# Early folds of the first batch's second row half on GpSimd, free PSUM banks for MLP groups, and transfers planned with other landings, in an attention and Fourier-mixing kernel on one core

## The chip, the cores and the metric

The kernel runs on one core of a Trainium2 chip. Such a core has five engines that run side by side, each with its own instruction queue and in its own order: TensorE (PE in the profile: matmuls, and PEld: its weight loads), VectorE (DVE), ScalarE (ACT), GpSimd (POOL) and SyncE (SP, which issues transfers). They wait for one another through semaphores. Transfers run on 16 DMA engines that all the queues share. Matrix products go into PSUM, which has eight banks per core; everything else lies in SBUF.

The metric is the time of one execution in device microseconds (us), shown as the median of several.

## The reference, cut to what matters

The inputs are `q`, `k`, `v` for 4 batches, 8 heads, 768 rows and 64 columns, memory keys and values of 8 rows for each head, and two MLP weights `w_ch1` (512 x 2048) and `w_ch2` (2048 x 512), all in float32.

```
for c in range(24):                      # chunks of 32 rows
    l, r = max(0, 32*c - 16), min(768, 32*c + 40)
    kk = concat(mem_k, k[:, :, l:r]); vv = concat(mem_v, v[:, :, l:r])
    a = softmax(q[:, :, 32*c:32*c+32] @ kk^T / 8)
    attn[:, :, 32*c:32*c+32] = a @ vv
x = attn as [4, 768, 512]
u = x + real(fft(fft(x, axis=1), axis=2))
un = (u - mean(u)) / sqrt(var(u) + 1e-6)          # over the 512 columns
out = u + relu(un @ w_ch1) @ w_ch2
```

So each batch goes through three stages: chunked attention, a two-dimensional discrete Fourier transform of which only the real part is kept, and a normalised MLP.

## The kernel before, in words

**Attention** (`attention(n)`) works on pairs of heads, four pairs to a batch, n = 0 to 15. For each pair GpSimd issues two transfers that load q and k and cast them to bf16 (`e_load_qk`, L324), into three buffers each (`qs`, `ks`); SP issues seven that load the values into one of four tiles `va` (`e_load_v`, L333, L337, L342). TensorE turns q and k with identity matmuls into PSUM (`turn`, L351; tiles `trq`, `trk`), ScalarE or, for k of the first batch, VectorE copies them out (`e_qT` L360, `e_kT` L379). Then, for two groups g of six 64-row blocks: scores (`e_scores`, L392, tile `sc`), exponentials (`e_exp`, L400, ScalarE), values with a column of ones for the sum (`e_values`, L416, tile `xa`, or `xo` in an MLP bank for g = 1 of the first batch), and division by the sum (`e_norm`, L426 and L427, VectorE), which writes rows 384g to 384g+383 of the pair's 128 columns of `xsb`, the batch's 768 x 512 result. With the pair order 0, 2, 1, 3 the columns c and 256 + c become ready early.

**The Fourier stage** uses symmetry: columns are folded (sums and differences of mirrored columns), the folded parts are split into an fp16 high part `hi` and a remainder `lo`, and products with cosine and sine tables transform the rows (tile `ps`) and then the columns (tile `pm`). The first batch has its own version, `first_fourier`, which starts on half the rows (g = 0: rows 0 to 383, g = 1: rows 384 to 767) before attention is complete. For each g and each parity `par`:

- `g_zy` (L556) adds or subtracts columns 0 to 127 and 256 to 383; it needs pairs 0 and 1 in order of work.
- `g_ff(..., last=0)` (L569, L571, L574), the early fold, twice per parity (`ab`), adds or subtracts the mirror of columns 128 to 255; it needs the third pair.
- `g_mid` (L600 to L603, GpSimd) prepares the middle columns; it needs the fourth pair. `g_row` (L608, L614) is its product.
- `g_ff(..., last=1)` (L573, L574), the last fold, with the fourth pair; then `g_hi` (L590, ScalarE), `g_lo` (L594, VectorE) and `g_rows` (L627, twelve matmuls).

`g_row(0)` is the first row transform that TensorE does. After g = 1 the results are copied out (`e_up` L500, `e_rest` L505, `e_dn` L513), `e_columns` (L638) transforms columns, `e_sum` (L644) adds x, `e_stats` (L652) and `e_un` (L658) normalise, and `e_turn_u` (L665) turns the result for the MLP. For the later batches (`fourier(b)`) GpSimd and SP send half of the rows through DRAM in mirrored order (`e_rows_out`, `e_rows_turn`, `e_mirror`), and SP turns the normalised rows by a transposing transfer (`e_flip`, L670).

**The MLP** takes half a batch (`sh`) at a time: 16 groups `e_ch1` (four matmuls into `ph`, L698), each followed by a ReLU on ScalarE (`e_relu`, L706), in order; then three groups `e_ch2` of 16 matmuls in four parts (`pc`, L713), and `e_osb` (L720) which adds u. The weights are eight GpSimd transfers (L906 for w1, L910 for w2), queued behind the loads of the sixth and the seventh head pair.

**PSUM.** The eight banks are handed out by name. The tags `acc` and `mlp` stand for two banks each; `tr`, `sc` (two banks) and `xa` hold the rest. Row and column transforms take `acc` (the first batch's rows of odd parity `mlp`). An MLP group has a fixed tag: `mtag` gives `acc` to every third one and `mlp` to the others.

**The order of the work** is made by a small planner, the class `Plan`, when the kernel is built. `add` notes a task with its engine, a cost in us, the tasks that it waits for (`after`, and `behind`: only issued later than that one), the buffers that it takes and gives back, and a rank. `order` then walks through a modelled time: whenever an engine is free, it takes the ready task of lowest rank. Without a rank given, a task's rank is its place in the list; MLP matmuls have a rank of a million and more, so they fill the holes of all other work. The result is a fixed order for each engine; on the chip an instruction waits for its real inputs, and everything behind it on its engine waits as well. Transfers with `moved` are modelled by `share`: the first transfer of each queue gets a share of the bandwidth, GpSimd's twice that of the others, and lands 2.8 us (GpSimd) or 1.4 us later, plus `late`.

While the first batch has no dense work for TensorE, the planner puts idle matmuls (`e_fill`, L771, operand `dz`) into its holes. A one-element copy, `e_gate` (L824), keeps GpSimd from issuing loads of the second batch before the fourth pair's values have landed.

GpSimd also prepares constants: zero rows of `kTb` (L777) and of `ks` (L754), masks, edges of `va` (L296 to L308). Their ranks run up to 17.1; those of the first three pairs' loads are given, up to 10.1, and the fourth pair's loads have their place in the list, which is higher than 20.

## Time and profile before

| quantity | value |
|---|---|
| median of 4 runs | 292.79 us (292.53 to 293.11) |
| the profiled execution's own time | 293.11 us |
| its span, first to last instruction | 291.4 us |
| PE busy, of the span | 94% |
| PE's first row transform (L608) | 32.44 us |
| PE's first MLP matmul (L698) | 55.12 us |
| PE's last matmul ends | about 287.2 us |

The span is what the trace shows; the device adds a little around it. A line of the order of time has the start and the duration in us, the engine, the line of the kernel, the operation, the result and its operands with their shapes, and how many were merged; in brackets how long the engine had been idle before it, and what ended that. A line of the waits has the waiting engine and line, what it waited for, the total in us, how often, and the longest. A line of the windows has the stretch, its length, then the busy time of PE, PEld, DVE, ACT and POOL with instruction counts, the granted clock, the DMA share and GB/s. Busy PE includes the idle matmuls of the start.

### The profile page before, as it was taken

How to read it: one execution, taken by the hardware profiler on the slowest of the kernel's cores; microseconds unless marked ns; L12 is line 12 of the kernel's file. 1: busy time of each engine (PE TensorE's matmuls, PEld its weight loads, DVE VectorE, ACT ScalarE, POOL GpSimd, SP SyncE). 2: the span in 40 equal slices, each digit the busy share in tenths (PEclk: the TensorE clock that was granted, in tenths of full speed). 3: DMA queues.
4: the chain of work that ended last, by engine and by line, in shares of the span. 5: the costliest groups of instructions: out<-in, count | busy, mean ns of one | idle time of the engine just before them, and what ended most of it. 6: DMA issues, size and time to landing. Idle time of an engine off the chain costs nothing.

```text
span 291.4 us, 7349 instructions
## 1 busy us (share of the span) xinstructions
PE 274.2 (94%) x3055; PEld 173.0 (59%) x3055; DVE 164.8 (57%) x354; ACT 164.7 (57%) x294; POOL 47.9 (16%) x96
## 2 busy tenths in 40 slices
PE   1599998998999999999999999999899999999994
PEld 1377697764566767566777646657554644645641
DVE  7979998941259874948885878864912012012011
ACT  5897356767576586877885246433750721712700
POOL 8824822310321010221010021010020000000000
PEclk9999999999999999999999999999999999999999
DMA  5998999997999967798940356944222504004204
GB/s 98 196 192 163 182 209 197 197 197 156 178 202 261 182 170 166 95 162 213 192 95 35 37 137 190 146 144 108 56 54 75 107 0 126 21 36 107 39 36 108
DMA packets 98689, 38.36 MB, mean 132 GB/s; under 512 B 85728, under 2 KB 93920, under 8 KB 98656
## 3 DMA queue, kind: packets, MB, share of 16 engines
q1 hardware_dynamic: 87344, 21.83, 39.9%
q0 software_dynamic: 10592, 15.21, 28.0%
q10 hardware_dynamic: 720, 0.85, 0.9%
q8 instruction: 24, 0.39, 0.6%
q14 instruction: 9, 0.07, 0.1%
HBM read 37.36 MB, written 13.37 MB: 174 GB/s over the span
## 4 chain that ended last, share of the span: by engine, by line
PE 78%; POOL 5%; DMA 5%; issue 4%; DVE 4%; SPq 2%; ACT 1%; POOLq 0%; DVEq 0%
PE pc L713 29%; PE ph L698 25%; PE xa L416 6%; PE ps L488 5%; PE pm L638 3%; DMA va<-in_mem_v_dram 3%; PE ps L627 2%; PE sc L392 2%; DMA qs<-in_q_dram 2%; SPq L333 2%; PE trq L351 2%; PE trk L351 2%; DVE st L652 1%; DVE xsb L644 1%; POOL qs L324 1%
## 5 line engine op out<-in xcount | busy, mean ns | idle before, releaser
L706 ACT ACTIVATE hT<-ph 128x384 f16<-128x384 f32 x128 | 60.8, 492 | 53.7 <-PE ph L698 52.8
L698 PE MATMUL ph<-unT,w_sb 128*128 128x384 f16 x512 | 88.9, 326 | 0.9 <-ACT hT L706 0.6
L713 PE MATMUL pc<-w_sb,hT 128*128 128x512 f16 x384 | 88.0, 380 | 0.0
L698 PEld LDWEIGHTS <-w_sb 128*128 128x128 f16 x512 | 48.4, 98 | 33.2 <-issue 1.8
L713 PEld LDWEIGHTS <-hT 128*128 128x128 f16 x384 | 35.8, 98 | 40.6 <-issue 0.4
L720 DVE SCALAR_TENSOR_TENSOR osb<-pc,rstd,xsb 128x512 f32<-128x512 f32 x24 | 18.0, 750 | 72.4 <-PE pc L713 69.7
L400 ACT ACTIVATE e<-sc,mbias 128x384 f32<-128x384 f32 x64 | 33.6, 578 | 10.6 <-PE sc L392 9.3
L416 PE MATMUL xa<-va,e 128*64 128x65 f32 x672 | 26.2, 228 | 0.8 <-DMA va<-in_mem_v_dram 0.8
L416 PEld LDWEIGHTS xa<-va,e 128*64 128x64 f32 x672 | 22.3, 139 | 7.8 <-issue 5.2
L658 ACT ACTIVATE un<-xsb,mu_s 128x512 f16<-128x512 f32 x24 | 17.2, 722 | 14.2 <-DVE mu_s L653 14.2
L500 ACT CAST up<-ps 128x386 f16<-128x386 f32 x16 | 9.7, 604 | 17.1 <-PE ps L488 15.6
L652 DVE BATCH_NORM_STATS2 st<-xsb 128x6 f32<-128x512 f32 x24 | 16.6, 690 | 0.7
L360 ACT COPY qT<-trq 128x768 bf16<-128x768 bf16 x16 | 12.7, 795 | 7.3 <-PE trq L351 7.3
L324 POOL DMA_DIRECT2D qs<-in_q_dram x16 | 10.6, 660 | 36.2 <-PE trq L351 22.9
L427 DVE TENSOR_TENSOR xsb<-xa,zs 128x384 f32<-128x384 f32 x28 | 15.6, 557 | 1.0
L505 DVE TENSOR_TENSOR up<-ps,up 128x386 f16<-128x386 f32 x16 | 9.5, 596 | 10.7 <-ACT up L500 10.7
L351 PE MATMUL trq<-ident_b,qs 96*64 96x96 bf16 x256 | 9.1, 218 | 6.7 <-DMA qs<-in_q_dram 6.7
L426 DVE RECIPROCAL zs<-xa 128x6 f32<-128x6 f32 x28 | 5.4, 191 | 17.1 <-PE xa L416 16.7
L379 ACT COPY kTb<-trk 128x1056 bf16<-128x1056 bf16 x12 | 12.5, 1040 | 2.2 <-PE trk L351 2.2
L324 POOL DMA_DIRECT2D ks<-in_k_dram x16 | 10.2, 640 | 20.8 <-PE trk L351 16.9
L644 DVE TENSOR_TENSOR xsb<-pm,xsb 128x512 f32<-128x512 f32 x15 | 10.1, 671 | 5.4 <-PE pm L638 5.4
L351 PEld LDWEIGHTS <-qs 96*64 96x64 bf16 x256 | 6.9, 116 | 10.1 <-DMA qs<-in_q_dram 7.6
(142 smaller groups left out, 331.2 us busy)
## 6 DMA issues: line engine op xcount, KB each, us to landing
va<-in_v_dram SPq DMA_DIRECT2D x32, 220.0 KB
w_sb<-in_moe_w_ch_dram POOLq DMA_DIRECT2D x8, 512.0 KB, 16.3
qs<-in_q_dram POOLq DMA_DIRECT2D x16, 192.0 KB, 6.0
ks<-in_k_dram POOLq DMA_DIRECT2D x16, 192.0 KB, 6.7
out_dram<-osb SPq DMA_DIRECT2D x12, 256.0 KB
x_rows<-xsb POOLq DMA_DIRECT2D x3, 768.0 KB, 5.0
xr<-x_back POOLq DMA_DIRECT2D x3, 768.0 KB, 5.3
out_rows<-osb SPq DMA_DIRECT2D x9, 256.0 KB
```

Source lines behind the costliest of these rows:

```text
L324: nc.gpsimd.dma_start(dst[n % NS][0:QP], src[b, 2 * pr:2 * pr + 2].rearrange("h (p j) d -> p h (j d)", j=RB))
L351: nc.tensor.transpose(out_[64 * hh:64 * hh + 64, j * w:(j + 1) * w], src[:, hh, j * D:(j + 1) * D], eye)
L400: nc.scalar.activation(e1[:, :, :, ts(half, 32)], sc[:, :, 0:6, ts(half, 32)], AFT.Exp, bias=mbias[:, half:half + 1], scale=1.0 / math.sqr ...
L416: nc.tensor.matmul(xa[64 * half:64 * half + 64, st, hh, 0:65], e1[:, hh, t6, :], v1[:, hh, 6 * g + t6, 0:65], start=True, stop=True)
L427: nc.vector.tensor_tensor(xs[b][:, 3 * g:3 * g + 3, 2 * pr * D:(2 * pr + 2) * D] .rearrange("p s (h d) -> p s h d", h=2), xa[:, :, :, 0:D] ...
L488: nc.tensor.matmul(out_[:, sp, :], part[:, ab, sp * 3 + st, c0:c1], tab[:, sp, st, :], start=(st == 0 and i == 0), stop=(st == 2 and i == 1))
L652: nc.vector.bn_stats(st6, xs[b][:, kt, :])
L658: nc.scalar.activation(un, xs[b][:, kt, :], AFT.Identity, bias=mu_of[b][:, kt, 0:1], scale=-1.0)
L698: nc.tensor.matmul(ph[:, 0:384], w1_sb[:, dt, ts(ht, P)], unT_of[b][:, dt, sh * 384:(sh + 1) * 384], start=(dt == 0), stop=(dt == NDT - 1))
L706: nc.scalar.activation(hT_of[b, sh][:, ht, :], ph[:, 0:384], AFT.Relu, bias=0.0, scale=-1.0)
L713: nc.tensor.matmul(pc_of[b, sh, stl], hT_of[b, sh][:, ht, ts(stl, P)], w2_sb[:, ht, :], start=(ht == 0), stop=(ht == NHT - 1))
L720: nc.vector.scalar_tensor_tensor(osb, pc, rstd_of[b][:, st:st + 1], xs[b][:, st, :], ALU.mult, ALU.add)
```

## The change: what it does

- **Early folds.** For g = 1, `g_zy` and `g_ff(..., last=0)` run on GpSimd: two `g_zy` and four early folds, with ranks 20.1 to 20.3 and costs of 1.1, 1.42 and 1.3.
- **Free banks.** An MLP group has no fixed tag. `order` picks, among `mlp` and `acc`, one that has a free bank, by how long it has been free.
- **Transfers.** `share` weighs each transfer by its own `grain` and slows small-grained ones to 0.85 beside others; `head` says after which part of its cost a transfer begins; `moved`, `late` and `grain` of value loads, weights, mirrored rows and outputs have new values. The transposing transfers `e_flip` are planned with a cost of 1.2 and a landing 1.6 later, and each goes behind the one before and no longer after it.
- **Tiles and a memset.** Two tiles `kU` (128 x 8 x 128, bf16) are new, and a GpSimd task `t_uz` with rank 20 and cost 0.4 that writes zeros to both.
- **A second way to load q and k**, with transposing transfers, for batches from `TURNED` on. `TURNED` is 9 and there are 4 batches.

```diff
     def __init__(self, slots):
-        self.free = dict(slots)
+        self.free = dict(slots, **{"": 0})
...
-            heads = [xs_[0] + [2.0 if q == "POOL" else 1.0] for q, xs_ in left.items() if xs_]
+            heads = [xs_[0] + [xs_[0][0]["grain"], q] for q, xs_ in left.items() if xs_]
             live = [h for h in heads if h[2] <= at + 1e-9]
             whole = sum(h[3] for h in live)
-            step = min([h[1] * whole / h[3] for h in live]
+            slow = {q: 0.85 if len(live) > 1 and xs_ and xs_[0][0]["grain"] < 0.05 else 1.0
+                    for q, xs_ in left.items()}
+            step = min([h[1] * whole / h[3] / slow[h[4]] for h in live]
...
-                    xs_[0][1] -= step * (2.0 if q == "POOL" else 1.0) / whole
+                    xs_[0][1] -= step * slow[q] * xs_[0][0]["grain"] / whole
...
-                    for tag in t["take"]:
+                    take = t["take"]
+                    if t["pick"] is not None:
+                        take += tuple(sorted((x for x in t["pick"]["of"] if self.free[x] > 0),
+                                             key=lambda x: (since.get(x, []) + [0.0])[0]
+                                             + t["pick"]["of"].index(x) * 0.5))[:1] or ("",)
+                    for tag in take:
                         need[tag] = need.get(tag, 0) + 1
...
-                        self.flow.setdefault(e, []).append([t, t["moved"], now + cost])
+                        self.flow.setdefault(e, []).append([t, t["moved"], now + cost * t["head"]])
...
-                        t["done"] = now + cost + self.LAG.get(e, 0.07)
+                        t["done"] = now + cost + (t["late"] or self.LAG.get(e, 0.07))
+                        if e == "SP":
+                            t["end"] = t["done"]
...
+    KR, KS, NKU = 16, 128, 2
+    kU = [spool.tile([P, RB, KS], BF16, name=f"kU{i}") for i in range(NKU)]
...
+    TURNED = 9
...
     def g_zy(par, g):
...
-        xb, sl = xs[0], slice(3 * g, 3 * g + 3)
-        nc.vector.tensor_tensor(zy_of[0, par][:, sl], xb[:, sl, 0:P], xb[:, sl, HD:HD + P],
+        xb, sl, eng = xs[0], slice(3 * g, 3 * g + 3), nc.gpsimd if g == 1 else nc.vector
+        eng.tensor_tensor(zy_of[0, par][:, sl], xb[:, sl, 0:P], xb[:, sl, HD:HD + P],
                                 ALU.add if par == 0 else ALU.subtract)
...
     def g_ff(par, ab, g, last):
...
+        eng = nc.gpsimd if g == 1 and not last else nc.vector
...
-    def mtag(b, i):
-        return "acc" if i % 3 == 2 else "mlp"
+    pick_of = {}
+
+    def pick(*key):
+        return pick_of.setdefault(key, dict(of=("mlp", "acc")))
...
-        ph_of[b, sh, ht] = ph = bank(mtag(b, ht), [P, 512], FP32, "ph")
+        ph_of[b, sh, ht] = ph = bank(pick(b, sh, ht)["tag"], [P, 512], FP32, "ph")
...
+    t_uz = add("POOL", 0.4, lambda: [nc.gpsimd.memset(kU[i], 0.0) for i in range(NKU)], rank=20)
...
         lv = add("SP", 2.5, lambda: e_load_v(n), [t_ones[n] if n < NV else None],
                  behind=t_x2.get(b - 2),
-                 take=("va",), moved=2.7, late=LATE if b else 0.0)
+                 take=("va",), moved=2.6, grain=0.031, head=0.4, late=(0.0, 4.0, LATE, LATE)[b])
...
-                w1_sb[:, dt, :], moe_w_ch1[ts(dt, P), :]), moved=2.55,
+                w1_sb[:, dt, :], moe_w_ch1[ts(dt, P), :]), moved=2.4, grain=0.32, late=2.0,
...
-                w2_sb[:, ts(g, 4), :], w2v[:, ts(g, 4), :]), moved=3.1,
+                w2_sb[:, ts(g, 4), :], w2v[:, ts(g, 4), :]), moved=2.6, late=2.0,
...
-                zy = add("DVE", 0.5, lambda par=par, g=g: g_zy(par, g),
+                early = ("DVE", "POOL")[g]
+                zy = add(early, (0.5, 1.1)[g], lambda par=par, g=g: g_zy(par, g),
                          [t_norm[0, g], t_norm[1, g], t_sines],
-                         take=("unT",) if g == 0 else ())
+                         take=("unT",) if g == 0 else (), rank=20.1 if g else None)
                 for ab in range(2):
-                    pre[par, ab, g] = add("DVE", 0.62 if ab == 0 else 0.5,
+                    pre[par, ab, g] = add(early, (0.62 if ab == 0 else 0.5) + 0.8 * g,
                                           lambda par=par, ab=ab, g=g: g_ff(par, ab, g, 0),
-                                          [zy, t_norm[2, g]],
+                                          [zy, t_norm[2, g]], rank=20.2 + 0.1 * par if g else None,
...
-                t_un[kt] = add("SP", 0.1, lambda kt=kt: e_flip(b, kt),
-                               [un, t_un.get(kts[i - 1]) if i else None],
-                               take=("unT",) if i == 0 else (), give=("un",), moved=0.8,
+                t_un[kt] = add("SP", 1.2, lambda kt=kt: e_flip(b, kt),
+                               [un], behind=t_un.get(kts[i - 1]) if i else None,
+                               take=("unT",) if i == 0 else (), give=("un",), late=1.6,
...
-                         take=(mtag(b, ht),), give=("unT",) if sh == 1 and ht == NHT - 1 else (),
+                         pick=pick(b, sh, ht), give=("unT",) if sh == 1 and ht == NHT - 1 else (),
```

## The prediction

> **What bounds the kernel now.** I read the page's busy shares first, then PE's waits, then windows by stage, then the order of time on PE and GpSimd from 7 to 33 us.
>
> ```profile
> PE 274.2 (94%) x3055; PEld 173.0 (59%) x3055; DVE 164.8 (57%) x354; ACT 164.7 (57%) x294; POOL 47.9 (16%) x96
> ```
>
> TensorE is busy for 94% of the span; no other engine passes 60%. The windows (PE busy first) say where the rest lies:
>
> ```profile
> 22.00:32.00 10.00, 9.70 (x204) 6.72 (x196) 9.36 (x25) 6.19 (x11) 5.77 (x13) 1.00 0.91 160
> 32.00:44.00 12.00, 12.00 (x159) 10.63 (x153) 11.49 (x32) 6.58 (x13) 5.82 (x10) 1.00 1.09 207
> 44.00:72.00 28.00, 26.07 (x390) 18.73 (x383) 17.33 (x42) 19.80 (x39) 4.84 (x8) 1.00 1.13 190
> 72.00:200.00 128.00, 128.00 (x1589) 81.76 (x1588) 90.20 (x170) 80.13 (x139) 15.74 (x22) 1.00 0.80 153
> 200.00:210.00 10.00, 9.11 (x65) 5.90 (x63) 7.82 (x18) 5.72 (x12) 0.00 (x0) 1.00 0.28 67
> ```
>
> From 32 us on TensorE has almost no gap: 1.93 us between 44 and 72, 0.89 between 200 and 210. Its waits from 30 us to the end name them:
>
> ```profile
> PE sc L392 <- ACT e L400: 0.8, 1, 0.8
> PE xa L416 <- DMA va<-in_mem_v_dram: 0.8, 1, 0.8
> PE ph L698 <- ACT hT L706: 0.6, 1, 0.6
> PE ph L698 <- DVE xsb L548: 0.3, 1, 0.3
> ```
>
> So two things count: when TensorE comes to its dense work, and these few waits. Before 32 us part of "busy" is idle filler (L771), and the dense work begins with the first row transform at 32.44. What leads there, in order of time on TensorE:
>
> ```profile
> 20.96 0.54 PE L351 MATMUL trq<-ident_b,qs 96*64 96x96 bf16 x16
> 21.32 0.54 PE L351 MATMUL trk<-turn_b,ks 100*64 100x100 bf16 x16
> 21.80 0.35 PE L392 MATMUL sc<-qT,kTb 64*128 64x64 bf16 x12
> 22.07 0.92 PE L416 MATMUL xo<-va,e 128*64 128x65 f32 x24
> ...
> 32.44 0.33 PE L608 MATMUL ps<-dz 128*128 128x386 bf16 x1
> ```
>
> The turns at 20.96 and 21.32 belong to the fourth head pair. GpSimd issues its loads here (with the memset rows that I price by):
>
> ```profile
> 7.30 0.78 POOL L777 MEMSET kTb<- 128x384 bf16 x2
> 9.33 1.99 POOL L754 MEMSET ks<- 4x1024 bf16 x2
> 14.97 0.13 POOL L308 MEMSET va<- 8x2 f32 x1
> 15.23 0.65 POOL L324 DMA_DIRECT2D qs<-in_q_dram  x1
> 15.88 0.63 POOL L324 DMA_DIRECT2D ks<-in_k_dram  x1
> ```
>
> Their landings, by tile, are 5.0 us (q) and 5.4 us (k) after issue: 20.2 and 21.28. So k arrives 0.04 us before TensorE turns it.
>
> **The change part by part.**
>
> *Dead code.* `TURNED = 9` with four batches: no branch on it runs, so the transposed q and k loads do not exist. What remains of it is two tiles, `kU`, and their memset, `t_uz`.
>
> *`t_uz` on GpSimd.* Rank 20 puts it behind the value-tile edges (17.1), which end at 15.10, and ahead of the fourth pair's loads, whose rank is their place in the list, far above 20. Nothing holds it back. It writes 128x1024 bf16 twice; the plan is told 0.4 us. By L754 (0.95 to 1.10 us for 1024 elements) the two take 1.9 to 2.2; by L777 (0.39 for 384) 2.1. A lower bound is VectorE's memset of `ks`, 0.485 for 1024 elements written as uint32: 0.97. I take 2.0, the same engine's row for the same length. The loads then go out at 17.23 and 17.88 and land at 22.2 and 23.3. TensorE, in order, turns k at 23.3 and not 21.32: +1.96. Behind it stand scores, values and 24 fillers whose number the plan, told 0.4, has no reason to change; ScalarE cannot hide it, since its exponentials wait 0.83 us each for `sc`. So the first row transform starts at about 34.4. Price: +1.96, all on the path.
>
> *Six early folds of rows 384 to 767 to GpSimd.* VectorE is rid of one fold at L556 (0.48, among three in 1.49) and of 2.6 us between 34.87 and 37.47: 3.1 together. On the path this is worth nothing, because TensorE is dense from 32.44 to 43.67 and would do no row transform sooner; the cover is gone only if that stretch had holes. On GpSimd no row shows a fold of 384 elements. From below: the iota at L276, 0.57 for 512 elements, so 0.43; from above: memset's 0.93 ns an element for two reads and a write, 1.27. I take 1.1, nearer the memset, as two inputs must be read. Six folds with two copies at 0.2 make 7.0 us. In the Trainium skill, "GPSIMD Engine Reference", section "Performance versus the Vector engine", a two-input add of 2048 elements takes 4.5 us; scaled, an estimate of 0.85 us, six of them 5.1 us.
>
> Queued behind them by rank and by the traced time of their inputs: two folds between the fifth pair's q and k, four among the sixth pair's and `g_mid`. The fifth pair's k goes from 26.67 to about 29 and lands by 35, turned at 39.15: hidden. `g_mid` has rank 20 and waits at most for one fold, 1.3; it comes after the norm, by then at 31.9, and has until 34.4: hidden. The sixth pair's k and all four w1 loads (28.54 to 30.7 now) move behind the last fold, to about 38 and 38.5 to 40.5. w1 lands 9.1 to 15.4 after issue now; with the longest figure the last is in by 56, and the first MLP matmul, now 55.12, stands at 57.1: hidden, with one microsecond to spare. w2 (34.5 to 40.5 now, 17 to 21.5 to land) follows to about 62 to 70, wanted from 71.8: hidden.
>
> *The two engines side by side.* `g_mid` shows it: 0.20, 0.18 and 0.20 us for its three instructions alone, then 0.44, 0.39 and 0.39 while VectorE folds. From these rows a fold loses 0.2, and VectorE nothing visible. The Trainium skill, "SBUF — State Buffer", section "Who interferes with whom", says more and speaks against the change: a VectorE instruction with two SBUF inputs and a GpSimd one that reads SBUF shut each other out for a whole instruction. By that, six folds of 1.1 could block VectorE for up to 6.6 us, more than the 3.1 taken off it, and the sum would be up to 4.8 higher. I take 0. The bounds from rows: 0, since TensorE's dense stretch lets no gain through, and +0.2, if VectorE lost 0.24 at each of the eight fold and copy instructions (1.9) against a slack of 1.75: the first `lo` is ready at 32.05 and used at 33.80.
>
> *Free bank choice.* Between 203 and 209 an MLP group bound to `acc` waits for a bank that a column group holds, and the ReLUs behind it are in order, so later groups clog `mlp`. With either bank this goes: −0.89, the window's idle; bounds 0 and −1.3 (matmul starts leave holes of 0.5 and 0.74 there as well as smaller ones). An MLP group may now sit on `acc` when a Fourier step wants it; 128 gapless microseconds of other MLP work cover that.
>
> *New landings and weights in the plan.* They only reorder. The 0.84 wait for values at 70.37 should go: TensorE comes 1.96 later and the value loads gain while w1 is not yet queued. The 0.85 for ScalarE at 45.4 and 0.23 at 52.46 are latency and stay. The transposes on SP are now chained by issue, not landing; no TensorE wait names them: 0. A new order also makes new waits; between 0 and the 1.93 that 44 to 72 now holds I take 0.5, about a quarter.
>
> *Sum:* 1.96 − 0.89 − 0.84 + 0.5 = +0.73 on the profiled execution, 293.11 with 291.4 of span; it stands 0.3 above the median, so 293.5.
>
> **The rivals.**
>
> *Faster: the memset costs little.* If GpSimd writes bf16 in pairs like VectorE (0.97 for both), the shift is 0.93; with no new wait the sum is −0.8; with no shift at all −1.7. So 291.1 to 292.0. It decides below 1.1 us of memset without new waits. For it: VectorE's row. Against: both GpSimd rows count 1024 and 384 bf16 elements, not half as many words.
>
> *Slower: the folds push w1 too far.* If a fold takes 1.6, GpSimd reaches w1 three microseconds later, the last lands at 59, and the first MLP group waits two: 293.5 + 2 = 295.5. It decides from about 1.3 a fold. For it: `g_mid` doubling beside VectorE. Against: with fewer loads ahead of it w1 should need less than 15.4.
>
> *Slower: TensorE cools.* It ran the same turns in 0.85 until 17.6 and in 0.53 after, so it is slow until it has been busy for a while. Two pauses (1.2 and 0.7 us) at 21 to 23.3 may undo that. The next scores, values and seven fillers would take 0.15 + 0.35 + 1.2 more: 295.2.
>
> *The change does nothing measurable:* shift and gains cancel, within the first case.
>
> **How the numbers follow.** The sum's case: 46%, 292.4 to 294.5; memset cheap: 26%; w1 late: 20%; cooling: 8%. A measurement of this kernel can tell about 0.2%, that is 292.2 and 293.4. Of the first case 25 points lie above, 20 within, 1 below; of the second 22 below, 4 within; of the third 18 above, 2 within; the fourth above. So slower 51%, same 26%, faster 23%. The likeliest is 293.5; 291.0 to 296.0 leaves a tenth at each end.
>
> **What would show it.** Two GpSimd memsets of 128x1024 ahead of the fourth pair's loads, about 1 us each; TensorE waiting near 21 us for q and k; the first row transform near 34.4; TensorE dense for 11 us after; no holes where columns of the last batch meet an MLP's first half; no value wait near 70. The prediction is wrong if the turn of the fourth k is not late, if folds take 1.6 or VectorE's folds stretch past TensorE, or if the first MLP group waits for w1.

## The result and the profile after

After: 293.69 us (median of 53 runs, 292.86 to 295.14). Before, in the same sessions: 292.94 us (79 runs). The ratio is 1.0024, 95% interval 1.0016 to 1.0032: slower by a quarter of a per cent, 0.7 us. The profiled execution took 294.24 us with a span of 292.5, against 293.11 and 291.4 before.

From the page, busy shares of the kernel after:

```profile
PE 276.6 (95%) x3060; PEld 174.2 (60%) x3060; DVE 166.5 (57%) x345; ACT 166.4 (57%) x294; POOL 57.9 (20%) x107
```

GpSimd has 10.0 us more (47.9 before): 2.05 of memset, the folds and their copies. VectorE, from which the folds were taken, has 1.7 us *more*, with nine instructions fewer. That is the first sign that its instructions became longer.

Windows of the kernel after (start and end, length, busy time of PE, PEld, DVE, ACT and POOL with instruction counts, granted clock, DMA share, GB/s):

```profile
22.00:32.00 10.00, 9.33 (x222) 6.88 (x215) 7.65 (x21) 6.72 (x12) 4.89 (x9) 1.00 0.92 159
32.00:44.00 12.00, 10.90 (x143) 8.60 (x140) 11.89 (x24) 5.29 (x11) 10.89 (x18) 1.00 1.01 167
44.00:72.00 28.00, 28.00 (x400) 20.73 (x398) 19.42 (x45) 21.00 (x37) 8.75 (x13) 1.00 1.16 200
72.00:200.00 128.00, 128.00 (x1630) 82.25 (x1629) 91.02 (x172) 82.94 (x144) 15.66 (x22) 1.00 0.76 151
200.00:210.00 10.00, 10.00 (x68) 6.30 (x67) 7.93 (x18) 5.14 (x11) 0.00 (x0) 1.00 0.44 91
```

The holes have moved. 44 to 72 is full (1.93 us missing before), 200 to 210 is full (0.89 missing before), but 32 to 44, which was full, now lacks 1.10. TensorE's waits of 0.2 us and more from 30 us to the end are a single line:

```profile
PE ps L667 <- DVE hl L634: 1.0, 1, 1.0
```

The early order on TensorE, kernel after (start, duration, engine, line, operation; in brackets the idle time before it):

```profile
16.61 0.88 PE L374 MATMUL trk<-turn_b,ks 100*64 100x100 bf16 x16 [0.61 <-DMA ks<-in_k_dram]
17.42 0.50 PE L432 MATMUL sc<-qT,kTb 64*128 64x64 bf16 x12
19.79 0.75 PE L374 MATMUL trq<-ident_b,qs 96*64 96x96 bf16 x16
...
23.25 0.53 PE L374 MATMUL trq<-ident_b,qs 96*64 96x96 bf16 x16
24.35 0.55 PE L374 MATMUL trk<-turn_b,ks 100*64 100x100 bf16 x16 [0.56 <-DMA ks<-in_k_dram]
...
35.20 0.33 PE L648 MATMUL ps<-dz 128*128 128x386 bf16 x1
```

In the kernel before, the lines for the first pair's second scores and the third pair's k are:

```profile
15.96 0.50 PE L392 MATMUL sc<-qT,kTb 64*128 64x64 bf16 x12
18.26 0.52 PE L351 MATMUL trk<-turn_b,ks 100*64 100x100 bf16 x16
```

The first row transform comes at 35.20 (32.44 before): 2.76 us late, not 1.96. The fourth pair's turns (23.25 and 24.35) are late as forecast. But above them stands something that the prediction did not have: at 16.61 TensorE turns the *third* pair's k, after a wait for its load, and only then does the first pair's second scores (17.42). In the kernel before, the scores came first. And the turn of q at 19.79 still takes 0.75 us, while it took 0.53 from 17.89 on before: TensorE stays at its slow pace for over two microseconds longer. This pace is seen in the durations alone; the granted clock of the profile reads 1.00 there.

GpSimd at that time, kernel after:

```profile
15.14 2.05 POOL L850 MEMSET kU<- 128x1024 bf16 x2
17.14 0.65 POOL L347 DMA_DIRECT2D qs<-in_q_dram  x1
17.78 0.63 POOL L347 DMA_DIRECT2D ks<-in_k_dram  x1
```

So the sum of the profiled executions: +2.76 (start) +1.01 (the wait for `hl`) −0.85, −0.23, −0.84 and −0.89 (all the waits of before) = +0.96, beside +1.1 of span. The sign and the size of the forecast came out, but four of its terms did not. So the agreement is in good part luck; the sum of the errors stands below. The experiments ask what lies behind each.

### The profile page after: what moved, and what is told of

Its sections match the earlier page's. It is cut to its first block, busy times and chain, and to the rows that moved or that the text cites. A ratio compares the mean times of both kernels' runs of the same rounds, so it can differ in the third digit from the quotient of the medians.

```text
span 292.5 us, 7361 instructions
## 1 busy us (share of the span) xinstructions
PE 276.6 (95%) x3060; PEld 174.2 (60%) x3060; DVE 166.5 (57%) x345; ACT 166.4 (57%) x294; POOL 57.9 (20%) x107
## 4 chain that ended last, share of the span: by engine, by line
PE 86%; POOL 5%; DVE 4%; DMA 2%; issue 1%; POOLq 0%
PE ph L740 29%; PE pc L755 29%; PE xa L455 7%; PE ps L527 5%; PE pm L678 5%; PE sc L432 2%; DMA ks<-in_k_dram 2%; PE trk L374 2%; PE ps L667 2%; PE trq L374 2%; DVE ff L614 1%; POOL qs L347 1%; DVE hl L634 1%; DVE xsb L466 1%; PE pm L578 1%
## 5 line engine op out<-in xcount | busy, mean ns | idle before, releaser
L748 ACT ACTIVATE hT<-ph 128x384 f16<-128x384 f32 x128 | 62.0, 491 | 51.3 <-PE ph L740 50.3
L740 PE MATMUL ph<-unT,w_sb 128*128 128x384 f16 x512 | 87.9, 326 | 0.0
L347 POOL DMA_DIRECT2D ks<-in_k_dram x16 | 10.3, 646 | 23.3 <-PE trk L374 22.6
L517 DVE TENSOR_TENSOR lo<-ff,hi 128x768 f16<-128x768 f32 x12 | 11.4, 954 | 3.7 <-ACT hi L512 3.6
```

The lines of the kernel that those rows point to most:

```text
L347: nc.gpsimd.dma_start(dst[n % NS][0:QP], src[b, 2 * pr:2 * pr + 2].rearrange("h (p j) d -> p h (j d)", j=RB))
L740: nc.tensor.matmul(ph[:, 0:384], w1_sb[:, dt, ts(ht, P)], unT_of[b][:, dt, sh * 384:(sh + 1) * 384], start=(dt == 0), stop=(dt == NDT - 1))
L748: nc.scalar.activation(hT_of[b, sh][:, ht, :], ph[:, 0:384], AFT.Relu, bias=0.0, scale=-1.0)
```

## The experiments

Each kernel is compared with the kernel before on the same chip, in ratios with 95% intervals. Edits are shown against the kernel after, unless said otherwise. "First row" is the start of the first row transform. Each kernel has one profile, and one profile is one execution: e6 below leaves TensorE's order ahead of the first row as it was and still shows it at 32.80, 0.36 later than the kernel before. Differences of that size between two profiles say little.

**1. The memset (e1_no_memset).** The planner still has the task, so the order is that of the kernel after; nothing is written.

```diff
-    t_uz = add("POOL", 0.4, lambda: [nc.gpsimd.memset(kU[i], 0.0) for i in range(NKU)], rank=20)
+    t_uz = add("POOL", 0.4, lambda: None, rank=20)
```

> The changed kernel with the same order on every engine, but without the two GpSimd memsets of kU. Theory M (the memset alone sets the late start, because it delays the fourth pair's loads): loads go out 2.0 us earlier, TensorE turns the fourth k 2 us earlier, the first row transform stands at 33.2 and the time falls by 2.0 to about 291.7. Rival T (the new order of TensorE, with the third pair's k turned ahead of the first pair's second scores, already costs 1.5 us, and the memset only what is on top): TensorE comes to the fourth q no sooner than 22.95, the first row transform stands at about 34.2, and the time falls by only 0.9 to 292.8.

Measured: 293.84 us, 1.0046 [1.0020, 1.0072]: not faster than the kernel after. From the order of time on PE:

```profile
16.63 0.88 PE L374 MATMUL trk<-turn_b,ks 100*64 100x100 bf16 x16 [0.70 <-DMA ks<-in_k_dram]
17.44 0.50 PE L432 MATMUL sc<-qT,kTb 64*128 64x64 bf16 x12
...
23.84 0.53 PE L374 MATMUL trk<-turn_b,ks 100*64 100x100 bf16 x16
...
34.67 0.33 PE L648 MATMUL ps<-dz 128*128 128x386 bf16 x1
```

Without the memset the fourth pair's k is issued at 15.79 and lands 5.2 us later, at 21.0; TensorE does not come to its turn before 23.84. Between these two profiles the memset moves the first row by only 0.53 us of the 2.76; the other 2.23 are there without it, with the early turn at 16.63. The two do not come to full pace at the same time (about 20.4 us in the kernel after, 21.9 here), so the split is rough. What the times say is firmer: without the memset the kernel is no faster.

**2. The memset alone (e5_memset_alone).** The kernel before, with `kU` and its memset (and the branches for `TURNED`, which never run).

```diff
+    t_uz = add("POOL", 0.4, lambda: [nc.gpsimd.memset(kU[i], 0.0) for i in range(NKU)], rank=20)
```

> The kernel before with only the memset task added (the order of the other engines is that of before). Theory C (the memset delays the fourth pair's k by 2.0 us, and the pause lets TensorE fall back to its slow clock, as the run with the old landings showed with seven fillers in 2.42 us): the fourth k is turned at 23.2, the seven fillers take 2.4 us, the first row transform stands near 35.6, and the time rises by about 2.3 us over before (3.2 less the value wait of 0.84). Theory M (only the delay counts): fillers in 1.3 us, first row transform at 34.4, the time 1.1 us over before.

Measured: 293.64 us, 1.0030 [0.9998, 1.0062], which does not tell it from no change. From the order of time on PE:

```profile
22.02 0.54 PE L370 MATMUL trk<-turn_b,ks 100*64 100x100 bf16 x16 [0.59 <-DMA ks<-in_k_dram]
...
32.77 0.33 PE L644 MATMUL ps<-dz 128*128 128x386 bf16 x1
```

The load went out at 17.64, 1.76 later than before, but was in after 4.3 us instead of 5.4. So the transfer caught up 1.1 of the delay, and the first row came only 0.33 later than before, within the scatter of single profiles. In the kernel after, the same load (issued at 17.78) took 6.5 us. A time from issue to landing is no fixed property of a load.

**3. The new landing model (e4_old_landings, e8_landings_alone).** In the first, the kernel after with the transfer model of before (shares, `moved`, `late`, and the `e_flip` chain):

```diff
-            heads = [xs_[0] + [xs_[0][0]["grain"], q] for q, xs_ in left.items() if xs_]
+            heads = [xs_[0] + [2.0 if q == "POOL" else 1.0, q] for q, xs_ in left.items() if xs_]
...
-                 take=("va",), moved=2.6, grain=0.031, head=0.4, late=(0.0, 4.0, LATE, LATE)[b])
+                 take=("va",), moved=2.7, late=LATE if b else 0.0)
```

> The changed kernel with the old model of transfers in the planner; memset, folds and banks as changed. Theory T: the second scores of the first pair are again ahead of the third pair's k, at 16.0 and not 17.4, so that only the memset's 2.0 us delay the start, the first row transform stands near 34.4, 0.8 sooner; the value wait of 0.8 at 70 us may come back, so the time lies between 292.9 and 293.7. Theory M: the start stays where it is, at 35.2, and the time stays or rises by 0.8 with the value wait, 293.7 to 294.5.

Measured: 293.91 us, 1.0043 [1.0018, 1.0067]. From the order of time on PE:

```profile
15.40 0.50 PE L428 MATMUL sc<-qT,kTb 64*128 64x64 bf16 x12
...
21.94 0.53 PE L370 MATMUL trq<-ident_b,qs 96*64 96x96 bf16 x16 [1.33 <-DMA qs<-in_q_dram]
23.23 0.55 PE L370 MATMUL trk<-turn_b,ks 100*64 100x100 bf16 x16 [0.77 <-DMA ks<-in_k_dram]
25.18 2.42 PE L809 MATMUL idle<-dz 128*128 128x384 bf16 x7
...
35.62 0.33 PE L644 MATMUL ps<-dz 128*128 128x386 bf16 x1
```

The clock row of its page (40 slices of the span, granted clock in tenths):

```profile
PEclk9997999999999999999999999999999999999999
```

The second scores are back at 15.40, so the model is what moved them. But the start is not back: the first row stands at 35.62, and not near 34.4. TensorE now comes early to the fourth pair, and the memset's delay shows as two pauses, 1.33 and 0.77 us. After them seven fillers take 2.42 us instead of the 1.31 of the kernels before and after, and the granted clock dips in the fourth slice. This is the forecast's rival "TensorE cools", in another kernel than the one it was priced for. Of its 12 runs 8 had a granted clock of 0.995 or less; of the kernel after none of 54.

In the second, the kernel before with the new landing model alone:

> The kernel before with only the new model of transfers in the planner. Theory T (the model lands the third pair's k too early, so that its turn is put ahead of the first pair's second scores and TensorE waits and stays slow for longer): second scores at 17.2 to 17.4, first row transform near 34.5, later waits for values near 70 us gone, and the time 1.2 us over before. Rival M (only the memset delays the start): first row transform near 32.5 and the time 0.8 us below before.

Measured: 297.26 us (5 runs), 1.0134 [1.0093, 1.0174], the slowest of all. From the order of time on PE:

```profile
16.33 0.54 PE L373 MATMUL trk<-turn_b,ks 100*64 100x100 bf16 x16 [0.86 <-DMA ks<-in_k_dram]
33.03 0.33 PE L647 MATMUL ps<-dz 128*128 128x386 bf16 x1
```

The third pair's turn is early here too, after a wait of 0.86 us, but TensorE is at full pace from this turn on (0.54 us), and the first row stands at 33.03, not near the 34.5 that theory T expected. So the early turn does not always bring the long slow pace. The longest waits of PE from 30 us on:

```profile
PE xa L454 <- DMA va<-in_mem_v_dram: 2.5, 1, 2.5
PE pm L677 <- DVE xsb L586: 2.3, 1, 2.3
```

The model by itself loses 4.5 us (297.26 against 292.8): a longer wait for values near 69 us, where theory T had expected none, with a granted clock of 0.57 behind it (70 to 74 us), and one of 2.3 between 200 and 210 us for VectorE's sums (L586), which the kernel before has only as 0.3.

**4. The third pair's turn (e9_k_later).** If the early turn is the cause of the late start, telling the planner that the third pair's loads land later must bring the start back. The kernel of experiment 1 with one number changed:

```diff
-                      ... late=LATE if b else 0.0,
+                      ... late=LATE if b else 2.4 if n == 2 else 0.0,
```

> The changed kernel without the two memsets, and with the planner told that the third pair's q and k land 2.4 us later, so that the first pair's second scores again go ahead of the turn of the third k. Theory T (this turn, and the slow clock that follows from it, is what makes the start late): second scores at 15.5, TensorE at full clock from 17.6, first row transform at 32.5 to 32.8 and not 34.7; the 1.0 us wait for hl stays; the time about 1.9 us below the run without the memsets, that is 0.5 to 1.0 us below before. Rival (the fourth pair's loads or the clock keep the start late whatever the order): first row transform after 34, the time within 0.5 us of the run without the memsets.

Measured: 292.21 us, 0.9966 [0.9941, 0.9991], faster than both kernels. Against experiment 1 one planned landing is worth 2.0 us by the medians (+1.32 and −0.66, each against the kernel before in its own session) and 0.8%, or 2.3 us, by the ratios. Its profiled execution was the one of 13 with a low granted clock (295.18 us, 0.987), so only the order is read from it: the second scores ran at 16.08, ahead of the turn at 18.22. That the start comes back is seen in experiment 8, where two kernels with the same planned landing have their first row at 32.08 and 31.95.

But not all of the 2.0 to 2.3 is the start, because that one number moved something else as well. From the order of time, on VectorE and then on PE:

```profile
40.00 2.61 DVE L634 TENSOR_TENSOR hl<-ff,hl 128x384 f16<-128x384 f32 x2
```

```profile
40.74 0.67 PE L654 MATMUL ps<-odd,mid 128*1 128x193 f16 x6
41.34 1.18 PE L667 MATMUL ps<-cosS,hl 128*128 128x193 f16 x12
```

The products of the middle columns for odd parity (twelve matmuls, 40.23 to 41.34) now stand ahead of those that need `hl`; in the kernel after and in experiment 1 they stand behind. VectorE's pair is as slow as ever (2.61 us), but TensorE has work meanwhile and does not wait for it, where theory T had expected the 1.0 us to stay. That leaves an estimate of 1.0 to 1.3 us for the start.

What does the early turn cost, then? Six profiles have it. In e8 and e11 TensorE is at full pace by about 17 us, and the first row stands at 33.03 and 33.75; in the kernel after, e1, e2 and e3 the slow pace lasts to between 20 and 23 us, and it stands at 34.41 to 35.20. Without the early turn, and without a fall of the clock behind it, it stands at 31.95 to 32.80 (five profiles), and the slow pace ends before 19. As a rough estimate from these, the order alone is worth about 1 us, and a slow pace that lasts longer another 1 to 2. That the early turn brings it on is likely, four of six against none of eight, but not shown: no kernel has more than one profile.

**5. The folds (e2_folds_back, e7_folds_alone).** The kernel after with all early folds on VectorE again:

```diff
-        xb, sl, eng = xs[0], slice(3 * g, 3 * g + 3), nc.gpsimd if g == 1 else nc.vector
+        xb, sl, eng = xs[0], slice(3 * g, 3 * g + 3), nc.vector
...
-        eng = nc.gpsimd if g == 1 and not last else nc.vector
+        eng = nc.vector
```

> The changed kernel with the six early folds back on VectorE, with their old costs and ranks; memset, banks and landings as changed. Theory L (VectorE and GpSimd shut each other out, so the folds on GpSimd cost TensorE the 1.0 us wait for hl at 39 us and win nothing): that wait goes and the time falls by about 0.8, to 292.9. Rival F (the folds on GpSimd are free and VectorE needs the relief): VectorE is 3 us later, TensorE waits for the second row half, and the time rises by up to 1, to 294.7.

Measured: 293.09 us, 1.0016 [0.9993, 1.0039], not to be told from the kernel after. PE's longest waits:

```profile
PE sc L432 <- ACT e L439: 0.8, 1, 0.8
PE xa L455 <- DMA va<-in_mem_v_dram: 0.5, 1, 0.5
```

The wait for `hl` is gone, and two waits of the kernel before are back. What made `hl` late is seen in the groups on VectorE from 30 to 46 us (count, busy time, mean ns of one), first of this kernel:

```profile
L634 DVE TENSOR_TENSOR lo<-ff,hi 128x384 f16<-128x384 f32 x4 | 2.1, 551 | 0.0
L634 DVE TENSOR_TENSOR hl<-ff,hl 128x384 f16<-128x384 f32 x4 | 2.1, 550 | 0.0
```

The kernel after:

```profile
L634 DVE TENSOR_TENSOR hl<-ff,hl 128x384 f16<-128x384 f32 x4 | 3.6, 945 | 0.0
L634 DVE TENSOR_TENSOR lo<-ff,hi 128x384 f16<-128x384 f32 x4 | 2.7, 686 | 0.0
```

The same instructions, 550 ns in one kernel, 945 and 686 in the other. The slow pair in the order of time of the kernel after, on VectorE:

```profile
38.57 2.61 DVE L634 TENSOR_TENSOR hl<-ff,hl 128x384 f16<-128x384 f32 x2
```

And what GpSimd does at that time:

```profile
38.19 2.57 POOL L614 TENSOR_TENSOR ff<-zy,xsb 128x381 f32<-128x381 f32 x2
```

Two VectorE subtractions, 1.02 us together when alone, take 2.61 us beside two folds of 2.57.

The folds moved in the kernel before, alone:

> The kernel before with only the six early folds moved to GpSimd. Theory L (exclusion): VectorE's instructions with two SBUF inputs stretch to twice their time or more where GpSimd folds, TensorE waits about 1 us for hl near 37 us, and the time is 0.5 to 1 us over before. Rival F (free): TensorE stays dense from 32.4 to 43.7 and the time is that of before within 0.3 us.

Measured: 294.61 us, 1.0055 [1.0021, 1.0090]. `hl` takes 945 ns here too, but TensorE, which comes later here (first row at 36.65), waits only 0.3 us for it. The profiled execution (298.23 us) had two pauses for the fourth pair, 0.77 and 1.40 us, with no memset in the kernel, and a granted clock of about half in the fourth slice (22 to 30 us) behind them; so such pauses need no memset.

**6. Reads or writes (e11_writes_only).** Do the folds slow VectorE because GpSimd is busy, or because it reads? The four mirrored additions on GpSimd are replaced by three memsets each of the same tile, which keep the engine busy as long:

```diff
+        if g == 1 and not last:
+            for _ in range(3):
+                eng.memset(ff[:, :, 1:P], 0.0)
+            return
```

> The changed kernel with the four mirrored adds of the early folds of the second row half left out; in the place of each GpSimd writes zeros to the same columns three times, about as long, and reads nothing. Theory L (VectorE's two-input instructions are shut out by a GpSimd instruction that reads SBUF): the split of hl takes 0.55 and not 0.95 on the mean, TensorE's 1.0 us wait for hl goes, and the time falls by 0.8 to 1.0 to about 292.8. Rival (any long GpSimd instruction beside it stretches VectorE, or the wait has another cause): hl stays at 0.9 or more and the wait at 1.0.

Measured: 292.46 us, 0.9983 [0.9958, 1.0007]. Groups on VectorE, 30 to 46 us:

```profile
L638 DVE TENSOR_TENSOR lo<-ff,hi 128x384 f16<-128x384 f32 x4 | 2.1, 550 | 0.0
L638 DVE TENSOR_TENSOR hl<-ff,hl 128x384 f16<-128x384 f32 x4 | 2.0, 549 | 0.0
```

Group on GpSimd, the same stretch:

```profile
L616 POOL MEMSET ff<- 128x381 f32 x12 | 4.9, 416 | 0.5
```

GpSimd works 4.9 us (4.8 with the folds), in the same places, and VectorE keeps its 550 ns; the wait for `hl` is gone. So it is not that GpSimd is busy: beside its writes VectorE loses nothing, beside its two-input additions it does. (The first `lo` pair, 33.98 to 35.00, lies wholly beside memsets, the `hl` pair in its second half. A memset is shorter than an addition, 0.42 us against 1.2; but neither subtraction is longer even by that.) The time is no clean price of the wait: the start came sooner in this profile as well, and a new one came up.

```profile
15.83 0.88 PE L374 MATMUL trk<-turn_b,ks 100*64 100x100 bf16 x16
33.75 0.33 PE L652 MATMUL ps<-dz 128*128 128x386 bf16 x1
```

The new wait is one of 1.5 us for q at 71.66.

**7. The banks (e3_fixed_banks, e6_banks_alone).** The kernel after with the fixed tags:

```diff
-        return pick_of.setdefault(key, dict(of=("mlp", "acc")))
+        return pick_of.setdefault(key, dict(of=("acc" if key[2] % 3 == 2 else "mlp",)))
```

> The changed kernel with the old fixed PSUM tags for MLP groups. Theory (the free choice closes the holes where the last batch's columns meet an MLP's first half): the holes of 0.9 us around 205 us come back, the time rises by 0.9 to 294.6. Rival (the new order alone moved the columns away from the holes): the same time, 293.7.

Measured: 294.79 us, 1.0072 [1.0051, 1.0093], 1.1 us above the kernel after by the medians, 1.4 by the ratios. PE's waits:

```profile
PE ps L667 <- DVE hl L634: 1.0, 1, 1.0
PE ph L740 <- ACT hT L748: 0.6, 1, 0.6
PE ph L740 <- DVE xsb L587: 0.3, 1, 0.3
```

The two last are those of the kernel before, 0.9 together. Free banks take them away.

The free choice in the kernel before, alone:

> The kernel before with only the free choice of PSUM banks for MLP groups. Theory (the choice closes the holes near 205 us and costs nothing): no waits of TensorE behind ReLU after 200 us, everything up to 55 us as before, and the time 0.9 us below before. Rival (MLP groups take acc from Fourier steps and open other holes): no change within 0.3 us.

Measured: 295.35 us, 1.0073 [1.0042, 1.0105]. PE's longest wait:

```profile
PE xa L450 <- DMA va<-in_mem_v_dram: 1.6, 1, 1.6
```

The holes after 200 us are gone here as well, but the wait for values near 70 us has doubled (0.84 to 1.6). Of its 12 runs 9 had a low granted clock; the profiled one had not, and took 293.59, and the other two without it 293.44 and 294.19. So a part that does what it says can still lose, and here most of the loss goes with the low clock. What brings the low clock on in this kernel is not shown.

**8. Why the wait for values goes (e10_k_later_no_folds, e12_w1_held).** The forecast put it down to the late start and to w1, which is not queued yet. The kernel of experiment 4 (e9), but with the folds on VectorE and no memset task, should then have an early start and no `hl` wait:

> As the run with the third pair's loads planned later and without memset, but the early folds back on VectorE: what is left of the change is the free banks and the landings. Theory L (the folds cost 1.0 us at hl and save only the 0.85 wait for exponentials at 45 us): no hl wait, that 0.85 wait back, the time equal to that with the folds within 0.4 us and below before by 0.8 to 1.5 us. Rival F (VectorE needed the relief): TensorE waits for the second row half and the time is over 0.8 us above the run with the folds.

Measured: 295.32 us, 1.0067 [1.0038, 1.0096]. First row at 32.08, no wait for `hl`, and yet 3.1 us slower than with the folds on GpSimd. Two of PE's waits:

```profile
PE xa L454 <- DMA va<-in_mem_v_dram: 2.0, 1, 2.0
PE ps L666 <- DVE lo L633: 0.5, 1, 0.5
```

The clock row of its page:

```profile
PEclk9999999998999999999999999999999999999999
```

The issue of w1 in the order of time on GpSimd:

```profile
28.65 2.17 POOL L957 DMA_DIRECT2D w_sb<-in_moe_w_ch_dram  x4
```

The wait for values is 2.0 us and half clock follows it (0.50 from 72 to 74 us). w1 goes out at 28.65; with the folds on GpSimd it goes out at 40 to 43, behind them in the queue. The last run tests that: the same kernel, where w1 is held back on GpSimd by a copy of one element. A second line of the edit puts the seventh pair's loads behind w1, where they stand in the kernel after as well.

```diff
+    def e_hold():
+        nc.gpsimd.tensor_copy(gate[0:1], ff_of[0, 0][0:1, 0, 3, 1:2])
...
-                behind=t_ck[n], rank=t_ck[n]["rank"] + 0.1) for dt in range(NDT))
+                behind=t_hold[0], rank=t_ck[n]["rank"] + 0.1) for dt in range(NDT))
...
-                      behind=t_gate if n == HP else t_xr[b - 2] if n == TURNED * HP else t_ck.get(n - 1),
+                      behind=t_gate if n == HP else t_xr[b - 2] if n == TURNED * HP else t_w1[3] if n == HP + 2 else t_ck.get(n - 1),
```

> The kernel of e10_k_later_no_folds (no kU and no memset, the third pair's q and k planned 2.4 us later, all early folds on VectorE, free banks, new landings) with one edit: a copy of one element on GpSimd that reads the last early fold of rows 384 to 767 stands ahead of the four w1 loads, and the loads of the seventh pair stand behind them, so that w1 goes out near 38 to 41 us, as it does where the folds are on GpSimd, and not at 28.65. Theory L (what the folds on GpSimd are good for is that they hold w1 back; issued early, its transfers take the DMA engines from the value loads): the wait for values near 68 us (2.0 us in e10_k_later_no_folds) and the half clock behind it are gone, no wait hl on VectorE's folds, first row transform at 32.1 to 33; time 290.6 to 291.8, ratio 0.993 to 0.997, that is 3.5 to 4.5 us less than the 295.32 of e10_k_later_no_folds and at or under e9_k_later (0.9966). Rival (the folds on GpSimd help in another way, by relieving VectorE, and the value wait has another cause): the wait near 68 us stays at 1.5 us or more and the time at 294.5 to 296. Rival (w1 held so late that the MLP starts late): a wait of TensorE for w1 near 55 us, 292.5 to 294.

Measured: 294.28 us, 1.0024 [0.9991, 1.0056], 1 us better than without the hold, which is not clear of the scatter, and not the 3.5 to 4.5 expected. PE's longest wait:

```profile
PE trq L373 <- DMA qs<-in_q_dram: 2.6, 2, 1.8
```

The issue of w1:

```profile
38.67 2.20 POOL L957 DMA_DIRECT2D w_sb<-in_moe_w_ch_dram  x4
```

w1 goes out at 38.67 and the wait for values is gone, as that theory has it. But TensorE now waits 2.6 us for q, in two places: 0.78 before 54.77 for the seventh pair's, which the edit itself moved (issued at 40.84, at 32.04 without the hold), and 1.77 before 70.65 for the eighth pair's, which took 19.2 us from issue to landing. In this kernel, holding w1 back decided *which* load came late, not whether one did.

All runs side by side. The load wait is TensorE's, for values or q, between 44 and 76 us; "low clock" counts timed runs with a granted clock of 0.995 or less. "Clock fell" marks profiles in which it dipped ahead of the first row.

| kernel | first row | load wait | wait for `e` at 45 | `hl` wait | low clock | ratio |
|---|---|---|---|---|---|---|
| before | 32.44 | 0.84 | 0.85 | – | 10 of 108 | 1 |
| after | 35.20 | – | – | 1.0 | 0 of 54 | 1.0024 |
| e1, no memset | 34.67 | – | – | 1.0 | 0 of 12 | 1.0046 |
| e2, folds back | 34.79 | 0.5 | 0.8 | – | 0 of 12 | 1.0016 |
| e3, fixed banks | 34.41 | – | – | 1.0 | 0 of 12 | 1.0072 |
| e4, old landings | 35.62 (clock fell) | – | – | 0.3 | 8 of 12 | 1.0043 |
| e5, memset alone | 32.77 | – | 0.8 | – | 4 of 12 | 1.0030 |
| e6, banks alone | 32.80 | 1.6 | 0.8 | – | 9 of 12 | 1.0073 |
| e7, folds alone | 36.65 (clock fell) | – | – | 0.3 | 2 of 12 | 1.0055 |
| e8, landings alone | 33.03 | 2.5 | 0.9 | – | 5 of 5 | 1.0134 |
| e9, third k later | 36.28 (clock fell) | – | – | – | 1 of 13 | 0.9966 |
| e10, same, no folds | 32.08 | 2.0 | 0.8 | – | 10 of 12 | 1.0067 |
| e11, writes only | 33.75 | 1.5 | – | – | 0 of 10 | 0.9983 |
| e12, same as e10, w1 held | 31.95 | 2.6 | 0.9 | – | 7 of 12 | 1.0024 |

The four parts alone (e5 to e8) cost 0.3, 0.7, 0.55 and 1.3%, all together 0.24%: their prices do not add. Beyond that, the table allows three readings. The wait for ScalarE's `e` at 45 us is there in all seven kernels with the folds on VectorE and in none of the seven with GpSimd busy in their place. The wait for *values* goes with w1: where w1 goes out at 28 to 29 us (before, e2, e5, e6, e8, e10), five of six profiles have it; where it goes out at 38.7 to 42.8, none of eight. And of the seven profiles whose first row lies before 34, six wait 0.8 to 2.6 us for a load; of the seven after 34, one does, for 0.5; the two that wait for q, e11 and e12, have w1 late and the first row early. The windows of the kernel after say why that may be: from 22 to 72 us the DMA share is 0.92 to 1.16 at 159 to 200 GB/s, from 72 to 200 us 0.76 at 151, so what TensorE gains at the start it meets again as a load that is not in. That is an association over fourteen profiles, with e5 as its exception; no run here slowed or sped up the transfers by themselves. The place of the folds divides the profiles about as well as the first row does (six of seven wait with the folds on VectorE, one of seven without), so the early start by itself is not shown to be the cause. Nor is it shown why e9 keeps its gain without such a wait, since its one profile is the execution with the low clock.

## Why the prediction was right, and where it was not

**The memset and the shift of the start (+1.96): the start was late, by 2.76, but for another reason.** The memset itself is as forecast, 2.05 us for 2.0 taken. What failed is the step from there to the path: "The loads then go out at 17.23 and 17.88 and land at 22.2 and 23.3", with the landing times of before added to a later issue. In the kernel before, with the memset alone, that load landed after 4.3 us (5.4 without it), and the start lost 0.33; in the kernel after it landed after 6.5 us, 1.0 later than forecast, but TensorE was late itself, and leaving the memset out gave back 0.53 of the start. In the times no price of the memset shows (e5 1.0030 [0.9998, 1.0062]; e1 no faster than the kernel after). The rival "the memset costs little" had the small price, but for another reason (packed writes, which the 2.05 us refute), and without what took its place.

**The new landings ("They only reorder"): this failed.** Priced at nothing on the start, they moved the third pair's turn ahead of the second scores, and TensorE, which was still slow, waited 0.61 us and stayed slow longer. Between the profiles this is 2.2 of the 2.76; from the times of experiment 4 we estimate 1.0 to 1.3 for the order at the start, and how much of the longer slow pace belongs to it stays open. The landing of that k was in the profile of before, but the forecast did not ask how a planner with other landings would order the first 20 us, where every task stands on the path.

**Folds: price right, "The two engines side by side ... I take 0" failed.** A fold takes 0.99 us alone and 1.2 on average (1.1 forecast). VectorE lost not 0.24 at an instruction but 0.8 at each of the pair at 38.57 (2.61 for 1.02), and TensorE waited 1.01 us behind it. The rows that the 0 rested on were of `g_mid`, with three elements a row and 0.2 to 0.4 us long, where a fold is 1.0 to 1.3. The Trainium skill, page "SBUF — State Buffer", section "Who interferes with whom", which was weighed and set aside, has the rule: a VectorE instruction with two inputs in SBUF contends with a GpSimd one that reads SBUF, and not with one that only writes. Here the measurements agree with both halves: 2.61 us for the pair beside folds, 549 ns each beside memsets. The 4.8 us worked out from it as an upper estimate was not reached: of the longer instructions only this pair made TensorE wait noticeably; the `lo` pair at 35.59, 1.58 us long, did not. The prediction named "VectorE's folds stretch past TensorE" as a sign that it is wrong; with `hl` that came to pass.

**New waits (+0.5): half.** After 30 us one came, of 1.01 us. It comes from VectorE's stretched subtractions (gone in e2 and e11); the order has a part in it too, since e9, with other products in front, does not wait.

**Free banks (−0.89): right.** The holes are gone, and 1.1 to 1.4 us come back with fixed tags.

**The wait for values (−0.84): right, the cause right in part.** The late start and the late w1 were both named. With w1 late, no profile waits for values. But where w1 is late and the start early (e11, e12), TensorE waits for q; so the late start seems to have its part in it.

**"The 0.85 for ScalarE at 45.4 and 0.23 at 52.46 are latency and stay": this failed.** Both went. The first goes with the folds off VectorE, in every kernel. So "On the path this is worth nothing" failed too: at 45 us, where the dense stretch has ended, the relief shows.

**w1 and w2: right.** w1 went out at 40.71 (38.5 to 40.5 forecast), and no wait names it (in e4, where it went out at 41.58, TensorE waited 0.3 us for it). The rival "the folds push w1 too far" did not happen; with w1 late the wait for values was gone.

**Cooling: not in this kernel, but real.** The price named, seven fillers 1.2 us longer after pauses of 1.2 and 0.7, is what e4 shows: 1.1 longer after 1.33 and 0.77.

By the terms of these profiles: +0.53 (memset), +2.23 (order, with the slow pace), +1.01 (`hl`), −0.89, −0.84, −0.85, −0.23 = +0.96, against the forecast's +0.73. Its errors nearly cancel: −1.43 on the memset, +2.23 for the order, +0.51 on the new wait, −1.08 for the two waits that were to stay. That the sum came within 0.23 us is therefore luck; the free banks, the wait for values and the duration of the memset were right on their merits.

## What to carry to other kernels

When a change gives a planner other transfer times, price the new order of the first stage, where everything is on the path, before any other term: here one planned landing was worth 2.0 to 2.3 us, by our estimate about half of it at the start and half because it put other work in front of a wait. Work moved from VectorE to GpSimd is not side by side if both read SBUF and VectorE's has two inputs; look for slack of a whole GpSimd instruction behind each. Where the DMA engines are full, test a gain at the start together with the loads that follow it: e6, e8 and e10, each with some of the parts, were slower than all of them together.

## What the runs showed of the hardware

- After two pauses of TensorE, 2.1 us in all between 20.6 and 23.2 us, its clock fell (e4: seven idle matmuls in 2.42 us instead of 1.31). The Trainium skill, page "TensorE: Matmul & The Clock Gate", section "Part 1: The HAM clock gate (the "warmup" mystery)", lets it fall after an idle window of about 3.4 us; here less idle time was enough. One pause of 1.08 us at the same place (e6, ahead of 22.05) was not.
- The same load of 192 KB, issued 1.76 us later, landed 4.3 us after its issue instead of 5.4, and 6.5 in a third kernel. Another load of 192 KB took 19.2 us where the engines were full (e12, issued at 51.38).
- Twelve GpSimd memsets beside VectorE's subtractions cost them nothing (549 ns); two-input additions in their place made them 945 ns.
